# Gated loop attention with a SoLU feed-forward: float64 weights converted in 7 wide pieces instead of 14, with a new written order

## The chip, the cores and the metric

The kernel runs on one core of a Trainium2 chip. The metric is device time in microseconds, the median of several executions. A profile covers one execution; its span runs from the first to the last instruction.

## The reference, cut to what matters

Two blocks, one behind the other. The first is a recurrence over 768 steps for 4 batches and 8 heads of size 48, with a complex decay; its output, (4, 768, 384) after the heads are put side by side, is the input x (3072 rows of 384) of the second. The inputs of the second block, w_in, w_out and g_ln, arrive as float64.

```python
a_re_n, a_im_n = (a_re * scale, a_im * scale)      # magnitude held to 0.999
for t in range(S):
    new_re = ar * S_re - ai * S_im
    new_im = ar * S_im + ai * S_re
    S_re, S_im = (new_re + kv, new_im)             # kv: outer product of k and v at t
    y[:, :, t] = np.einsum('bhd,bhde->bhe', q[:, :, t], S_re)
...
h = x @ w_in                                       # (3072, 384) @ (384, 1024)
e = np.exp(h - h_max)
solu = h * (e / (np.sum(e, axis=-1, keepdims=True) + 1e-09))
ln = (solu - mu) / np.sqrt(var + 1e-06) * g_ln
return (ln @ w_out).astype(np.float32)             # (3072, 1024) @ (1024, 384)
```

## The kernel before

The work is cut into 24 chunks of 128 rows (6 stretches of time by 4 batches), taken in 12 groups of two. A fast path (`whole`, line 614) computes everything and a set of conditions; a flag of one number is read at the end (line 1289), and only if it is set a slower general program (`general`, line 57) runs as well. In the profile it does not run.

Each piece of work is a named step, and the text ORDER (line 515) lists all steps, name and number, in the order in which they are written into the program. Since every engine takes its instructions in the order written, ORDER fixes each engine's queue: a step that waits holds up all that is written behind it on its engine. Most steps give work to one engine:

- SP, the DMA queue: `load_ar`, `load_ai`, `load_q`, `load_k`, `load_v`, `load_vr` (inputs of a group), `fetch` (a piece of raw weights), `gain` (g_ln), `last` and `onward` (small rows carried on, lines 866 and 921), `kqt0` (line 972, four DMAs that finish the transpose of a chunk's k and q), `away` (line 1128, the same for the feed-forward's activations), `store`, and `again` (a second fetch of a piece).
- VectorE (DVE): `ratio`, `tangent`, `size`, `lnm`, `ks`, `qs`, `on`, the first half of `part`, `k2`, `q2`, `kqb` (block transpose), `mask0`, `add`, `solu0`, `blocks`, `convert`, `centre`, `inspect`, and `judge`, `judgew`, `judges`, `flag`.
- ScalarE (ACT): `inverse`, `sure`, `square`, `secant`, `fourth`, `eps`, `grow`, `decay`, `angle`, `nearest`, `sin`, `cos`, the table loads `trig` and `exp`, `turned_x`, `exp0`, `spread`, `scale`, `tot`, `raised`, the copies `kT`, `qT`, `zT` and the copy in `meansum`.
- TensorE (PE): `total` (f_L) and `phase`, both at line 852; `score`, `values` (f_y), `carry` (f_d), `up` (f_h, with w_in), `down` (f_o, with w_out), `mean` and `meansum`, the transposes `qt`, `kt`, `zt`, and `turn_ends` and `count`.
- GpSimd (POOL): `centred` and `norm`.

A group's chain is: load, inverse ... lnm, total, grow and decay, a table load, angle, phase, nearest, part, sin and cos, then for each of its chunks k2, q2, kqb, kqt0, score, mask0, values, turned_x, up, exp0, solu0, blocks, away, down, scale, store. Chunks 0, 1, 2 and 23 use TensorE transposes in place of some of the DMAs.

The weights: `weight_steps` (line 724) cuts w_in (128 partitions, 3 blocks of 1024 columns) and w_out (8 blocks of 384) into 14 pieces, 0 to 5 of 512 columns of w_in (0, 1, 2 the first halves) and 6 to 13 the blocks of w_out. `fetch` brings the 64-bit words into a ring of 6 raw tiles. `raised` (ScalarE, line 750) takes the low words into a tile `bits`, of which there are two; `convert` (VectorE, lines 756 to 760) makes float32 from the high words and `bits` with three instructions. `mean` needs every converted block of w_out, `centre` (line 784) rewrites w_out with g_ln and that mean, and `down` needs the centred blocks. Near the end `again` fetches every piece a second time into the same ring and `inspect` (line 763) takes the least magnitude of each, a column of `least`; `judgew` counts them. `judge` takes one tile of the ring as scratch.

## Time and profile before

| | us |
|---|---|
| median of 3 runs | 434.31 |
| lowest and highest run | 432.13, 434.33 |
| the profiled execution | 434.73 |
| its span | 432.9 |
| TensorE busy in the span | 385.3 (89%) |
| VectorE busy | 334.9 (77%) |
| ScalarE busy | 289.0 (67%) |
| GpSimd busy | 54.1 (12%) |

TensorE's busy time counts its matmuls, which are pipelined, with modelled ends, so a busy TensorE need not be at its peak. A row of a timeline gives start, length, engine, line, operation, output <- inputs and shapes, and in brackets the idle time of the engine before it with what ended it. In a row of waits the figures are the total, the number of times and the longest. "PE f_o L1166 x8" in the chain of waits stands for eight instructions of that line which the chain passes through.

### The profile page before, as it was taken

What the parts mean: (1) busy time and instruction counts of PE and PEld (TensorE: products, weight loads), DVE (VectorE), ACT (ScalarE), POOL (GpSimd) and SP (SyncE); (2) the same over time, 40 slices, a digit from 0 to 9 for tenths busy, and PEclk for the clock granted to TensorE, in tenths of its full rate; (3) what the DMA queues carried; (4) which work ended last, traced back from release to release, by engine and by line L of the source; (5) the groups of instructions that cost most, each with busy time, mean ns of one, the idle gap of its engine ahead of it and who ended that gap; (6) DMA issues with size and microseconds to landing.
All of it is one profiled execution on the core that took longest, in us unless ns stands there. A gap on an engine that the chain in (4) does not pass through costs nothing.

```text
span 432.9 us, 15841 instructions
## 1 busy us (share of the span) xinstructions
PE 385.3 (89%) x6928; PEld 216.6 (50%) x6928; DVE 334.9 (77%) x457; ACT 289.0 (67%) x475; POOL 54.1 (12%) x139
## 2 busy tenths in 40 slices
PE   0257697899999999999998999999999999999991
PEld 0024163555644554554644745545555777667550
DVE  3898979798697799698887697979787897971381
ACT  4998965897579578667676487865874866522340
POOL 3000100103003021011021021031022030120210
PEclk9999889999999999999999999999999999999996
DMA  9999476686776767947877689968868869689761
GB/s 210 277 243 198 116 104 143 141 138 150 179 136 144 172 144 175 191 89 153 174 143 154 169 166 210 179 135 194 161 135 190 163 144 198 140 212 283 218 202 34
DMA packets 168126, 72.59 MB, mean 168 GB/s; under 512 B 142576, under 2 KB 155888, under 8 KB 168048
## 3 DMA queue, kind: packets, MB, share of 16 engines
q1 hardware_dynamic: 167904, 71.17, 75.2%
q8 instruction: 56, 0.92, 0.9%
q10 hardware_dynamic: 144, 0.33, 0.3%
q14 instruction: 22, 0.18, 0.1%
HBM read 38.87 MB, written 4.72 MB: 101 GB/s over the span
## 4 chain that ended last, share of the span: by engine, by line
PE 58%; DVE 13%; DMA 12%; SPq 7%; ACT 5%; issue 3%; DVEq 0%; ACTq 0%
PE f_h L1089 19%; PE f_o L1166 19%; PE f_y L1048 7%; PE f_score L1015 5%; DMA f_raw<-in_moe_w_in_dram 4%; DVE f_kb L970 3%; PE f_phase L852 3%; SPq L1131 3%; PE f_d L1056 2%; DMA f_kqT<-f_kb 2%; SPq L975 2%; PE f_L L852 2%; DMA f_v<-in_v_dram 2%; DMA f_zT<-f_zb 2%; DVE f_kq L961 2%
## 5 line engine op out<-in xcount | busy, mean ns | idle before, releaser
L1166 PE MATMUL f_o<-f_w_out,f_zT 128*32 128x384 f32 (+1 forms) x1344 | 130.2, 486 | 2.7 <-DVE f_w_out L784 2.5
L1089 PE MATMUL f_h<-f_w_in,f_xT 128*32 128x512 f32 x1152 | 131.5, 593 | 1.2 <-ACT f_xT L1082 1.2
L1166 PEld LDWEIGHTS f_o<-f_w_out,f_zT 128*32 128x32 f32 (+1 forms) x1344 | 60.9, 114 | 62.1 <-issue 41.9
L1089 PEld LDWEIGHTS f_h<-f_w_in,f_xT 128*32 128x32 f32 x1152 | 47.3, 110 | 59.5 <-issue 53.2
L970 DVE STREAM_TRANSPOSE f_kb<-f_kq 128x1536 f32<-128x1536 f32 x22 | 55.4, 2518 | 2.4 <-DMA f_kqT<-f_kb 2.1
L1048 PE MATMUL f_y<-f_att,f_v 128*32 128x128 f32 (+1 forms) x384 | 37.9, 273 | 3.2 <-DMA f_v<-in_v_dram 1.8
L1082 ACT COPY f_xT<-f_y 128x384 f32<-128x384 f32 x24 | 11.4, 477 | 41.8 <-PE f_y L1048 41.8
L1015 PEld LDWEIGHTS f_score<-f_kqT 96*32 96x32 f32 x1536 | 33.5, 111 | 10.7 <-issue 9.3
L1108 DVE SCALAR_TENSOR_TENSOR f_z<-f_h,f_z 128x1024 f32<-128x1024 f32 (+1 forms) x36 | 33.7, 971 | 5.4 <-ACT f_z L1099 5.4
L1099 ACT ACTIVATE f_z<-f_h 128x1024 f32<-128x1024 f32 x24 | 29.3, 1219 | 11.5 <-PE f_h L1089 11.5
L1048 PE MATMUL f_y<-f_att,f_vr 128*32 128x128 f32 x384 | 36.8, 273 | 0.0
L1015 PE MATMUL f_score<-f_kqT 96*32 96x96 f32 (+3 forms) x1536 | 35.0, 236 | 0.7 <-ACT f_kqT L988 0.6
L1048 PE MATMUL f_y<-f_kqT,f_state 96*32 96x128 f32 (+1 forms) x640 | 34.3, 272 | 0.0
L852 PE MATMUL f_L<-f_lr,f_mats 128*32 128x384 f32 x192 | 20.0, 518 | 15.7 <-DMA f_vr<-in_v_dram 13.8
L1144 POOL TENSOR_SCALAR f_less<-f_sum 128x1 f32<-128x1 f32 x24 | 11.7, 489 | 174.1 <-DVE f_z L1108 173.8
L1020 DVE TENSOR_TENSOR f_att<-f_score,f_mats 128x1024 f32<-128x1024 f32 x24 | 29.2, 1216 | 5.1 <-PE f_score L1015 5.0
L1048 PEld LDWEIGHTS f_y<-f_att,f_v 128*32 128x32 f32 (+1 forms) x384 | 23.4, 103 | 12.8 <-issue 6.9
L1147 ACT ACTIVATE f_z<-f_z,f_less 128x1024 f32<-128x1024 f32 x24 | 27.4, 1143 | 1.7 <-POOL f_less L1144 1.6
L907 DVE SCALAR_TENSOR_TENSOR f_f<-f_f,f_phase 128x384 f32<-128x384 f32 x24 | 12.6, 552 | 18.9 <-ACT f_f L903 18.7
L852 PE MATMUL f_phase<-f_x,f_mats 128*32 128x384 f32 x192 | 21.0, 546 | 5.3 <-ACT f_x L890 5.3
L961 DVE TENSOR_TENSOR f_kq<-f_cs,f_k 128x768 f32<-128x768 f32 x24 | 22.8, 950 | 3.0 <-ACT f_cs L919 2.0
L1126 DVE STREAM_TRANSPOSE f_zb<-f_z 128x1024 f32<-128x1024 f32 x20 | 24.7, 1235 | 0.1
(101 smaller groups left out, 592.4 us busy)
## 6 DMA issues: line engine op xcount, KB each, us to landing
f_kqT<-f_kb SPq DMA_DIRECT2D x88, 192.0 KB, 3.6
f_zT<-f_zb SPq DMA_DIRECT2D x80, 128.0 KB, 3.2
f_raw<-in_moe_w_in_dram SPq DMA_DIRECT2D x12, 512.0 KB, 6.0
f_raw<-in_moe_w_out_dram SPq DMA_DIRECT2D x16, 384.0 KB, 5.3
f_q<-in_q_dram SPq DMA_DIRECT2D x12, 384.0 KB, 6.6
f_k<-in_k_dram SPq DMA_DIRECT2D x12, 384.0 KB, 4.9
f_v<-in_v_dram SPq DMA_DIRECT2D x12, 384.0 KB, 5.9
out_dram<-f_ot SPq DMA_DIRECT2D x24, 192.0 KB, 3.9
```

The costliest lines, as they stand in the source:

```text
L852: nc.tensor.matmul(out=ps[r:r + 32], lhsT=weights[:, r:r + 32], rhs=st[nm][:, i * DM:(i + 1) * DM], start=True, stop=True)
L961: nc.vector.tensor_tensor(out=t, in0=T["cs", g][:, i * H:(i + 1) * H], in1=heads(T[nm, g][:, i]).unsqueeze(2).to_broadcast([P, H, 2, D]), ...
L970: nc.vector.transpose(out=t, in_=T["kq", c].rearrange("p n h (f j) -> p j (n h) f", j=3))
L1015: nc.tensor.matmul(out=scores[r0:r0 + 32, x, r:], lhsT=QK[:, r // 32, x], rhs=QK[:, r // 32:, H + x], start=True, stop=True)
L1020: nc.vector.tensor_tensor(out=st["att"].rearrange("p (i u) t -> p i u t", u=2), in0=scores.rearrange("p (i u) t -> p i u t", u=2), in1=mat ...
L1048: nc.tensor.matmul(**product)
L1089: nc.tensor.matmul(out=st["h"][r:r + 32, half * 512:(half + 1) * 512], lhsT=st["xT"][:, c * P + r:c * P + r + 32], rhs=w_in[:, c, half * 5 ...
L1099: nc.scalar.activation(out=z, in_=h, func=AF.Exp, accum_out=sums[:, n:n + 1])
L1108: nc.vector.scalar_tensor_tensor(out=z, in0=h, scalar=1.0, in1=z, op0=OP.mult, op1=OP.mult, accum_out=st["sum"][:, 2 + i:3 + i])
L1126: nc.vector.transpose(out=st["zb"], in_=st["z"].rearrange("p (c s f) -> p s c f", s=4, f=32))
L1147: nc.scalar.activation(out=st["z"], in_=st["z"], func=AF.Square, bias=st["less"], accum_out=st["sum"][:, 1:2])
L1166: nc.tensor.matmul(out=st["o"][rows], lhsT=zT, rhs=w_out[:, c], start=(c == 0), stop=(c == KF - 1))
```

## The change

The 14 pieces become 7: pieces 0 to 2 are the whole blocks of w_in (1024 columns), 3 to 6 are pairs of blocks of w_out (768 columns, fetched by two DMAs into the two halves of one tile). The ring has 3 tiles of twice the size, and there is one `bits` tile of twice the size, so the memory is the same. `least` has 7 columns and `inspect` runs 7 times. ORDER is another text: not only the places of `fetch`, `raised`, `convert`, `again` and `inspect` are new, but also those of many other steps through the whole program.

```diff
-    rawp, bits = pool("f_raw", 6), pool("f_bits", 2)
+    rawp, bits = pool("f_raw", 3), pool("f_bits", 1)
...
-        NW = 512
+        NW = 1024
         pieces = []
-        for w, src, nk in ((w_in, moe_w_in, KD), (w_out, moe_w_out, KF)):
+        for w, src, nk, per in ((w_in, moe_w_in, KD, 1), (w_out, moe_w_out, KF, 2)):
             wide = src.bitcast(I32).rearrange("(c p) w -> p c w", p=P)
-            nf = w.shape[2]
-            for f0 in range(0, nf, NW):
-                for c in range(nk):
-                    pieces.append((w, wide, c, f0, min(NW, nf - f0)))
+            for c in range(0, nk, per):
+                pieces.append((w, wide, c, per, per * w.shape[2]))
 
         def fetch(i):
-            w, wide, c, f0, n = pieces[i % len(pieces)]
-            raw = rawp.tile([P, NW, 2], I32, tag="raw", name="f_raw")[:, 0:n]
-            rows = wide[:, c, 2 * f0:2 * (f0 + n)]
-            if w is w_out:
-
-                rows = rows.rearrange("(s f) x -> f s x", s=4)
-            nc.sync.dma_start(out=raw.rearrange("p n u -> p (n u)"), in_=rows)
-            T["raw", i] = raw
+            w, wide, c, per, n = pieces[i % len(pieces)]
+            raw = T["raw", i] = rawp.tile([P, NW, 2], I32, tag="raw", name="f_raw")[:, 0:n]
+            for k in range(per):
+                rows = wide[:, c + k]
+                if w is w_out:
+
+                    rows = rows.rearrange("(s f) x -> f s x", s=4)
+                m = n // per
+                nc.sync.dma_start(out=raw[:, k * m:(k + 1) * m].rearrange("p n u -> p (n u)"), in_=rows)
...
-            hi, x = T["raw", i][:, :, 1], w[:, c, f0:f0 + n].bitcast(I32)
+            hi, x = T["raw", i][:, :, 1], w[:, c:c + per].rearrange("p c w -> p (c w)").bitcast(I32)
```

The order, engine by engine, where the prediction speaks of it (steps of other names left out):

```diff
 SP, first 45 us
-fetch:0 fetch:10 fetch:1 fetch:4 load_vr:0 fetch:3 load_q:0 load_k:0 fetch:2 load_ar:1 load_ai:1 fetch:5 fetch:11 fetch:9 fetch:7 gain:0 load_v:0 fetch:13 fetch:12 last:0 load_k:1 load_q:1 load_v:1 fetch:6 fetch:8 onward:0
+fetch:5 fetch:1 load_k:0 fetch:0 load_q:0 fetch:2 load_vr:0 load_ar:1 load_ai:1 fetch:6 last:0 load_v:0 fetch:3 fetch:4 gain:0 onward:0 load_k:1 load_q:1 load_ar:2
 SP, groups 6 to 8
-kqt0:12 away:10 load_vr:6 load_k:7 load_v:6 kqt0:13 last:7 store:8 store:9 onward:6 away:11 ... kqt0:14 load_vr:7 away:12 onward:7 load_k:8 load_v:7 kqt0:15 ... kqt0:16 onward:8 away:14 load_vr:8 load_k:9 load_v:8 kqt0:17
+kqt0:12 store:6 load_vr:6 away:10 load_v:6 load_k:7 store:8 kqt0:13 last:7 onward:6 away:11 ... kqt0:14 onward:7 store:10 away:12 load_vr:7 load_v:7 load_k:8 load_ar:9 kqt0:15 ... kqt0:16 load_vr:8 away:14 load_v:8 load_k:9 kqt0:17 onward:8
 DVE, up to mask0:1
-sizea:0 convert:10 lnma:0 convert:1 convert:0 qs1:0 convert:3 ks1:0 part0:0 ks0:0 qs0:0 part1:0 convert:4 k2:0 q2:0 k2:1 q2:1 ratio:1 convert:11 tangent:1 mask0:0 convert:2 size:1 convert:5 convert:13 convert:12 lnm:1 convert:9 convert:7 ks1:1 qs0:1 ks0:1 qs1:1 solu0:0 convert:6 part1:1 part0:1 convert:8 mask0:1
+sizeb:0 convert:5 lnmb:0 convert:1 ks1:0 convert:0 part0:0 qs0:0 qs1:0 part1:0 ks0:0 q2:0 k2:0 q2:1 convert:2 k2:1 ratio:1 mask0:0 tangent:1 convert:6 size:1 convert:3 lnm:1 convert:4 ks1:1 ks0:1 qs0:1 solu0:0 part0:1 part1:1 mask0:1
 ACT, from exp:1 to the copy of the mean
-exp:1 meansum:0 inverse:2 zT1:0 turned_x:1
+exp:1 zT1:0 inverse:2 turned_x:1 meansum:0
 PE, from carry:1 to phase:2
-carry:1 score1:1 zt1:0 mean:0 mean:3 score0:1 mean:4 mean:2 ... mean:5 meansum:0 values:1 zt0:0 turn_ends:1 carry:0 up1:1 up0:1 down0:0 score1:2 score0:2 total1:2 down1:0 total0:2 values:2 zt1:1 zt0:1 carry:2 phase1:2
+carry:1 phase0:1 phase1:1 score1:1 score0:1 zt1:0 mean:0 mean:1 mean:3 values:1 mean:7 ... mean:6 turn_ends:1 meansum:0 carry:0 up0:1 zt0:0 up1:1 score0:2 score1:2 down0:0 total1:2 total0:2 down1:0 values:2 zt0:1 carry:2 phase1:2
 DVE, the end
-solu0:23 inspect:10 inspect:7 inspect:6 inspect:12 judges:0 inspect:9 inspect:5 judge:0 inspect:4 inspect:1 judgew:0 flag:0
+solu0:23 inspect:1 inspect:3 inspect:0 judgew:0 flag:0
```

181 lines of the change are left out of this document (89 added, 92 removed).

## The prediction

> **What bounds the kernel now.** I read first the busy time by stage, then the chain of waits, then the timeline around the weight conversion and at the end. The stages, with columns PE, PEld, DVE, ACT, POOL busy, granted clock, DMA share and GB/s:
>
> ```profile
> 0.00:13.70 13.70, 0.00 (x0) 0.00 (x0) 5.63 (x18) 7.87 (x16) 3.48 (x11) 1.00 0.96 240
> 13.70:70.00 56.30, 38.67 (x518) 18.62 (x518) 50.56 (x89) 46.07 (x81) 1.54 (x4) 0.94 0.84 176
> 70.00:85.00 15.00, 11.52 (x192) 7.17 (x196) 13.21 (x22) 12.05 (x20) 1.90 (x6) 1.00 0.65 132
> 85.00:235.00 150.00, 149.84 (x2819) 78.77 (x2814) 124.71 (x149) 109.68 (x180) 20.73 (x52) 1.00 0.74 154
> 235.00:335.00 100.00, 97.49 (x1938) 53.82 (x1934) 80.77 (x95) 68.81 (x111) 14.51 (x31) 1.00 0.80 170
> 411.00:432.90 21.90, 11.74 (x90) 6.70 (x82) 10.24 (x31) 5.92 (x8) 1.80 (x7) 0.83 0.38 120
> ```
>
> From 85 us on TensorE is the bound: 0.16 us idle in 150. What a reordering can win lies where TensorE idles: 13.7 us before its first matmul, 17.6 us in the stage that holds the conversions (56.30 less 38.67), 3.5 us from 70 to 85 (15.00 less 11.52), 2.5 us from 235 to 335, and the end. Between 13.7 and 70 VectorE is the fullest engine (50.56 of 56.30), so conversion instructions there are near the path.
>
> The stage from 235 to 335 costs more than its idle time says, as the chain shows (start, length, what):
>
> ```profile
> 87.05 5.20 PE f_h L1089 x48
> ...
> 209.62 2.56 PE f_h L1089 x21
> ...
> 324.76 7.39 DMA f_v<-in_v_dram
> ...
> 336.98 2.63 PE f_h L1089 x22
> ```
>
> These are the first matmuls with w_in of chunks 2, 10 and 18: eight chunks took 122.6 us, the next eight 127.4. 4.8 us more for the same matmuls, and the chain names a load of v just ahead of the end of it.
>
> **The change part by part.**
>
> Conversion and inspection, per instruction:
>
> ```profile
> L750 ACT ACTIVATE f_bits<-f_raw x14: 539/601/712, 14.3 to 52.2; 128x384 int32<-128x384 uint32 x8, 128x512 int32<-128x512 uint32 x6
> L763 DVE TENSOR_REDUCE f_least<-f_raw x14: 541/606/760, 384.8 to 422.4; 128x1 f32<-128x384 f32 x8, 128x1 f32<-128x512 f32 x6
> ...
> L756 DVE TENSOR_SCALAR f_w_out<-f_raw x8: 352/352/358, 15.0 to 55.9; 128x384 int32<-128x384 int32 x8
> L758 DVE SCALAR_TENSOR_TENSOR f_w_out<-f_raw,f_w_out x8: 557/560/566, 15.3 to 56.3; 128x384 int32<-128x384 int32 x8
> L756 DVE TENSOR_SCALAR f_w_in<-f_raw x6: 417/420/425, 17.0 to 39.5; 128x512 int32<-128x512 int32 x6
> L758 DVE SCALAR_TENSOR_TENSOR f_w_in<-f_raw,f_w_in x6: 691/693/720, 17.4 to 39.9; 128x512 int32<-128x512 int32 x6
> ```
>
> From 384 to 512 columns L756 grows by 68 ns, 0.53 ns a column, with 0.15 us fixed; L758 by 133 ns, 1.04 ns a column, with 0.16 us fixed. The third instruction (L760) I take like L758. So a piece of 512 costs 0.42+0.69+0.69 = 1.81 us, one of 384 1.47, and by the same slopes (estimates, the sizes are not in this trace) 768 costs 0.56+0.96+0.96 = 2.48 and 1024 costs 0.69+1.22+1.22 = 3.14. All conversions: 6 x 1.81 + 8 x 1.47 = 22.6 before, 3 x 3.14 + 4 x 2.48 = 19.3 after, 3.3 us less on VectorE. If the larger forms have no fixed part to save it is 0. On ScalarE, 14 instructions between 0.54 and 0.71 become 7 that I estimate at 0.85 and 1.05: about 1.9 us less. Of the 14 inspections (0.54 to 0.76), near the end, 7 are left, each twice as wide: about 1.2 us less.
>
> DMAs: a w_in piece is now one transfer of twice the size, a w_out piece two transfers as before, so both rounds together issue 22 instead of 28. It moves the same bytes. In the first 13.7 us the DMA engines are 0.96 busy at 240 GB/s with the small pieces, so I put the bandwidth gain at 0. The Trainium skill (DMA: Bandwidth & Descriptors, Rules for kernel authors) asks for at least 1 MiB a transfer, and puts about 2.0 us of fixed time on each (Anatomy of one DMA); were that paid in series, the three w_in transfers that go would be worth 6 us and the sum would be lower by that. By the 0.96 row that time is already overlapped, so the sum holds nothing of it.
>
> *Up to the first w_in matmul: 0.* Before, what stands on VectorE ahead of what feeds up:0 is conversions 10, 1, 0, 3, 4, 11, 2: two of 384 and five of 512, 11.99 us. After, it is 5, 1, 0, 2: 2.48 + 3 x 3.14 = 11.90. The chain of group 0 beside them (total, grow, phase, k2, q2, scores, mask) has the same steps. So the start of up stays:
>
> ```profile
> 39.28 1.07 PE L1089 MATMUL f_h<-f_w_in,f_xT 128*32 128x512 f32 x8 [1.16 <-ACT f_xT L1082]
> ```
>
> The unknowns are the new waits. The ring is three tiles, so fetch:2, 6, 3 and 4 wait for conversions 5, 1, 0 and 2. SP is in order: behind fetch:2 stand load_vr:0, load_ar:1, load_ai:1; behind fetch:6 last:0 and load_v:0; behind fetch:4 gain, onward:0, load_k:1, load_q:1 and load_ar:2. And there is one bits tile, so each raised on ScalarE waits for the convert before it; behind raised:1 stand grow, decay, trig and angle of group 0. The tightest is raised:1. In the old run the second half of group 0 gets its size and its eps here:
>
> ```profile
> 14.48 0.56 DVE L840 SCALAR_TENSOR_TENSOR f_lr<-f_u,f_lr 128x384 f32<-128x384 f32 x1 [0.77 <-ACT f_u L833]
> 15.72 0.61 ACT L844 ACTIVATE f_u<-f_u,f_bias 128x384 f32<-128x384 f32 x1
> ```
>
> In the new order convert:5 follows that size: 15.04 + 2.48 = 17.5. On ScalarE raised:5 (0.85) is put ahead of eps, and fourthb comes behind it before raised:1: 16.33 + 0.85 and a little = 17.2 to 17.9. So raised:1 asks for the tile about when it comes free; for the later ones the same walk finds VectorE up to 1.8 us early. I take 0; the bounds are -2 (half of the 3.3 us saved there and some of the fetch issues) and +5 (two waits of a whole conversion of 2.5).
>
> *From there to 70 us: 0.* Left to convert after up:0's inputs are 1.81 + 6 x 1.47 = 10.6 before and 3 x 2.48 = 7.4 after. Before, the last one ends among the phase steps of group 1, and mask0:1 waits for score0:1, which in PE's order stands behind matmuls of the mean, and these wait for it:
>
> ```profile
> 56.88 0.56 DVE L760 CUSTOM_DVE_ANT_0 f_w_out<-f_w_out,f_bits 128x768 uint16<-128x768 uint16 x1
> 59.03 1.22 DVE L1020 TENSOR_TENSOR f_att<-f_score,f_mats 128x1024 f32<-128x1024 f32 x1 [1.59 <-PE f_score L1015]
> ```
>
> After, all conversions stand ahead of part0:1, and score0:1 ahead of every mean; mask0:1 can start near 56.2, 2.8 us earlier. But the next w_in matmuls do not follow it, for ScalarE loads its table for exp:1 (first row; the second is that matmul):
>
> ```profile
> 58.20 1.28 ACT L950 ACT_TABLE_LOAD   x1
> ```
>
> ```profile
> 64.05 0.62 PE L1089 MATMUL f_h<-f_w_in,f_xT 128*32 128x512 f32 x1
> ```
>
> That load is not moved, and the new order puts zT1:0, inverse:2 and turned_x:1 ahead of the copy of the mean, so I find up0:1 near 64 again. The lead is lost here.
>
> *70 to 85 us: -2.4.* The old chain:
>
> ```profile
> 75.97 0.73 PE f_L L852 x8
> 76.69 2.78 PE f_o L1166 x8
> 79.47 0.83 PE f_L L852 x8
> 81.21 1.28 ACT L947
> 82.60 0.66 issue
> 83.77 0.88 PE f_d L1056 x48
> 84.65 1.32 PE f_phase L852 x16
> ```
>
> Half of the running sums of group 2 (f_L) stood behind down1:0 (2.78 us), and both halves go before the table load, the angle and the phase matmuls. The new order has total1:2 and total0:2 together ahead of down1:0, so the phase comes up to 2.8 us earlier while down1:0 fills TensorE. I take off 0.4 for a wait that opens before zt0:1. Bounds 0 and -3.5, the stage's whole idle time.
>
> *85 to 335 us: -1.5.* Waits of TensorE for others in this stretch, and ScalarE's at its worst place:
>
> ```profile
> PE f_y L1048 <- DMA f_v<-in_v_dram: 1.8, 2, 1.2
> ```
>
> ```profile
> 244.14 1.05 ACT L903 ACTIVATE f_f<-f_phase,f_bias 128x384 f32<-128x384 f32 x2 [3.74 <-DMA f_on<-f_f]
> ```
>
> In the old SP order load_v stood behind load_k of the next group (groups 6 to 9), which nobody needs so soon; in the new one load_v goes ahead, so v lands one transfer sooner. And onward:6, for whose transfer ScalarE waited 3.74 us, no longer stands behind store:9, and store:8 has gone ahead of kqt0:13. I take 1.5 of the 4.8 us, most of the named 1.8. The rest of the order is new as well and no row prices it: bounds -4.8 (all gone) and +4.8 (as much again).
>
> *The end: -0.2.*
>
> ```profile
> 423.87 0.34 SPq L1175 DMA_DIRECT2D out_dram<-f_ot  x1
> 424.01 0.14 DVE L1223 TENSOR_SCALAR flag<-f_total 1x1 int32<-1x1 f32 x1
> ```
>
> Before, the last inspection waits for its fetch, and the flag is ready at 424.15, next to the last store, which is issued at 423.87 after matmuls that the change leaves alone. After, only inspections 1, 3 and 0 (about 3.3 us) stand behind solu0:23 on VectorE, so the flag comes with or before the store. The store hides what more is saved.
>
> Sum: 434.73 (the profiled execution; span 432.9 and 1.83 around it) - 2.4 - 1.5 - 0.2 = 430.63. That execution is 0.42 above the median of the runs, 434.31, so I predict **430.2 us**.
>
> **The rivals.** *The lead is used up* (no change). The slow stage may be set by VectorE, SP and transfers that take their time in turn and not by TensorE; then its excess grows from 4.8 by the 2.4 won before: 434.31 - 0.2 = 434.1. For it: VectorE is 81 of 100 us busy there, and the chain passes through transfers. Against: TensorE is still 97.5 of 100.
>
> *Single buffering bites* (slower). If VectorE runs more than about 2 us behind my walk, ScalarE stops at raised, SP at fetch, and what stands behind them goes late. Two such stops of a whole conversion (2.5 to 3.1 us) are 5.4: 434.3 - 2.6 + 5.4 = 437.1. It decides where those margins, 0 to 1.8 us, are used up. For it: VectorE is 50.56 of 56.30 busy. Against: conversions are 3.3 us shorter. The Trainium skill (Trainium Kernel Development and Optimization, Best Practices) asks to double-buffer so that DMA and compute overlap, and the change goes from six and two tiles to three and one; by that rule this rival is the outcome.
>
> *Onward comes late* (slower). In the new SP order onward:1, 4, 5, 6, 8 and 9 stand behind the second kqt0 of their own pair of chunks, where before only onward:6 did. The one 3.74 us wait stood at the head of the 4.8 us excess. If two more such waits come, 434.3 - 2.6 + 9.6 = 441.3. It decides when the transfer lands after the next group's phase matmuls. Against: those matmuls stand behind a whole down and values, so I find the transfer about level with them.
>
> **How the numbers follow.** About 0.5% (2.2 us) is what a measurement of this kernel can tell from no change: faster is below 432.1, slower above 436.5. Forecast, with its own range of 427 to 432.1: 0.53. Lead used up: 0.22. Single buffering: 0.13. Onward late: 0.12. The first alone is faster and the last two are slower: 0.53, 0.22, 0.25. The lower end is 426.5: the forecast with the bounds -3.5 and most of -4.8. The upper end takes in the lead used up and single buffering, 437.5; the late onward and a little below the range are left out.
>
> **What would show it.** Right: 7 groups of conversions near 2.5 and 3.1 us; first w_in matmul at 39 to 40; chunk 1's between 63 and 65; phase of group 2 near 82; first w_in matmuls of chunk 2 near 84.5 instead of 87.05; chunks 10 to 18 in about 126; flag before the last store. Wrong: waits of f_bits for L760 above 1 us, SP idle at L743 in the first 45 us, the first w_in matmul later than 41, waits of L903 for f_on at more than one place, or TensorE idle over 3 us between 85 and 411.

## The result and the profile after

| | before | after |
|---|---|---|
| median of 6 runs, us | 434.05 | 423.58 |
| lowest and highest run | 432.13, 434.60 | 421.44, 424.28 |
| the profiled execution | 434.73 | 421.44 |
| its span | 432.9 | 419.1 |

The ratio is 0.9757 (95% interval 0.9724 to 0.9789): 10.5 us faster, where 4.1 were predicted. The time lies under the lower end of the range, 426.5. The two profiled executions are 13.3 us apart, since that of after is 2.1 us under its median; the last experiment looks at what goes with that.

The same stages of the changed kernel, with the columns PE, PEld, DVE, ACT, POOL, granted clock, DMA share, GB/s; the last row is again the last 21.9 us:

```profile
0.00:13.70 13.70, 1.05 (x8) 0.20 (x8) 6.24 (x20) 8.89 (x18) 3.48 (x11) 1.00 0.93 248
13.70:70.00 56.30, 39.20 (x584) 20.31 (x581) 52.99 (x74) 49.33 (x80) 0.61 (x3) 0.94 0.78 185
70.00:85.00 15.00, 14.99 (x239) 7.28 (x242) 12.46 (x21) 11.70 (x19) 3.54 (x7) 1.00 0.68 145
85.00:235.00 150.00, 149.81 (x2822) 79.83 (x2817) 124.98 (x149) 109.73 (x181) 23.85 (x53) 1.00 0.71 159
235.00:335.00 100.00, 100.00 (x2066) 54.19 (x2063) 84.52 (x97) 72.35 (x116) 15.59 (x33) 1.00 0.78 171
397.20:419.10 21.90, 14.62 (x118) 6.90 (x110) 6.60 (x18) 5.40 (x8) 2.56 (x9) 0.94 0.43 153
```

TensorE no longer idles from 70 to 85 (14.99 of 15, before 11.52) nor from 235 to 335 (100.00, before 97.49). From 13.7 to 70 it is hardly busier, 39.20 against 38.67, yet it does 584 matmul records instead of 518 in that time.

Four rows of its timeline answer to those of before: the first w_in matmuls of chunk 0, the phase of group 1, ScalarE's table load for exp:1, and the first w_in matmul of chunk 1.

```profile
38.86 5.36 PE L1085 MATMUL f_h<-f_w_in,f_xT 128*32 128x512 f32 x48 [0.35 <-ACT f_xT L1078]
...
50.16 1.50 PE L848 MATMUL f_phase<-f_x,f_mats 128*32 128x384 f32 x16 [1.08 <-ACT f_x L886]
...
55.03 1.28 ACT L946 ACT_TABLE_LOAD   x1
...
60.80 0.62 PE L1085 MATMUL f_h<-f_w_in,f_xT 128*32 128x512 f32 x1
```

The first stands where it stood (39.28 before); the table load has gone from 58.20 to 55.03 and the last row from 64.05 to 60.80. In the chain of waits chunks 2 and 18 begin w_in here:

```profile
80.04 5.15 PE f_h L1085 x48
...
324.96 2.57 PE f_h L1085 x22
```

Before it was 87.05 and 336.98. With "up n" for the first w_in matmul of chunk n, read from each trace, the stretches are:

| stretch | before | after | change | predicted |
|---|---|---|---|---|
| start to up 0 | 39.3 | 38.9 | -0.4 | 0 |
| up 0 to up 1 | 24.8 | 21.9 | -2.8 | 0 |
| up 1 to up 2 | 22.8 | 19.1 | -3.8 | -2.4 |
| up 2 to up 18 | 249.9 | 244.9 | -5.0 | -1.5 |
| up 18 to the last scale | 86.5 | 87.2 | +0.7 | 0 |
| last scale to the end of the span | 9.7 | 7.1 | -2.5 | -0.2 |

Two of these changes depend on which executions are compared. With the same instructions on the way, up 0 to up 1 took 24.0 to 24.8 us in the four traces with 14 pieces and the old start, and 21.9 to 23.1 in the five with seven pieces and the new one; up 2 to up 18 took 247.3 to 249.9 in five traces with the old order there and 244.8 to 248.1 in eight with the new. So the two gains lie anywhere from 0.9 to 2.9 us and from nothing to 5. Up 1 to up 2 is steady in the new order, 18.9 to 19.1 us wherever the edit does not touch it.

The conversions themselves came out as estimated. By instruction (min/median/max in ns):

```profile
L746 ACT ACTIVATE f_bits<-f_raw x7: 892/949/1160, 13.0 to 43.5; 128x768 int32<-128x768 uint32 x4, 128x1024 int32<-128x1024 uint32 x3
L752 DVE TENSOR_SCALAR f_w_out<-f_raw x4: 550/554/556, 13.6 to 44.3; 128x768 int32<-128x768 int32 x4
L754 DVE SCALAR_TENSOR_TENSOR f_w_out<-f_raw,f_w_out x4: 957/959/982, 14.2 to 44.9; 128x768 int32<-128x768 int32 x4
L754 DVE SCALAR_TENSOR_TENSOR f_w_in<-f_raw,f_w_in x3: 1224/1225/1226, 17.3 to 29.4; 128x1024 int32<-128x1024 int32 x3
```

0.55 and 0.96 us for 768 columns (estimated 0.56 and 0.96), 1.225 for 1024 (estimated 1.22). ScalarE's `raised` is up to 0.1 longer than estimated (0.85 and 1.05), so it saves 1.1 us in all and not 1.9.

### The profile page after: what moved, and what is told of

It is laid out like the page before. It is cut to its first block, busy times and chain, and to the rows that moved or that the text cites. A ratio compares the mean times of both kernels' runs of the same rounds, so it can differ in the third digit from the quotient of the medians.

```text
span 419.1 us, 15795 instructions
## 1 busy us (share of the span) xinstructions
PE 381.9 (91%) x6928; PEld 200.4 (48%) x6928; DVE 331.8 (79%) x429; ACT 287.5 (69%) x468; POOL 57.0 (14%) x139
## 4 chain that ended last, share of the span: by engine, by line
PE 79%; ACT 9%; DMA 4%; DVE 3%; issue 2%; SPq 0%; POOL 0%; DVEq 0%; ACTq 0%; POOLq 0%
PE f_o L1162 28%; PE f_h L1085 26%; PE f_y L1044 9%; PE f_score L1011 5%; PE f_phase L848 4%; PE f_L L848 4%; PE f_d L1052 3%; DMA f_ar<-in_a_re_dram 2%; DMA f_raw<-in_moe_w_out_dram 1%; DMA f_kqT<-f_kb 1%; PE f_zt L1112 1%; ACT f_cs L912 1%; ACT L946 1%; DVE f_kb L966 1%; ACT f_cs L907 1%
## 5 line engine op out<-in xcount | busy, mean ns | idle before, releaser
L1162 PEld LDWEIGHTS f_o<-f_w_out,f_zT 128*32 128x32 f32 (+1 forms) x1344 | 55.0, 114 | 64.9 <-issue 55.0
L1085 PEld LDWEIGHTS f_h<-f_w_in,f_xT 128*32 128x32 f32 x1152 | 39.7, 110 | 64.8 <-issue 64.0
L1044 PE MATMUL f_y<-f_att,f_v 128*32 128x128 f32 (+1 forms) x384 | 36.1, 273 | 1.2 <-DVE f_att L1016 1.2
L1140 POOL TENSOR_SCALAR f_less<-f_sum 128x1 f32<-128x1 f32 x24 | 13.1, 546 | 163.4 <-DVE f_z L1104 152.7
L1011 PE MATMUL f_score<-f_kqT 96*32 96x32 f32 (+3 forms) x1536 | 32.8, 236 | 0.0
L1044 PE MATMUL f_y<-f_kqT,f_state 96*32 96x128 f32 (+1 forms) x640 | 32.7, 272 | 0.0
L1166 ACT ACTIVATE f_ot<-f_o,f_rs 128x384 f32<-128x384 f32 x24 | 13.7, 573 | 16.5 <-POOL f_rs L1151 6.0
L1044 PEld LDWEIGHTS f_y<-f_att,f_v 128*32 128x32 f32 (+1 forms) x384 | 21.8, 103 | 6.2 <-issue 3.8
L1122 DVE STREAM_TRANSPOSE f_zb<-f_z 128x1024 f32<-128x1024 f32 x20 | 24.8, 1238 | 0.1
L957 DVE TENSOR_TENSOR f_kq<-f_cs,f_q 128x768 f32<-128x768 f32 x24 | 22.9, 952 | 2.2 <-ACT f_cs L912 1.1
```

The lines of the kernel that those rows point to most:

```text
L957: nc.vector.tensor_tensor(out=t, in0=T["cs", g][:, i * H:(i + 1) * H], in1=heads(T[nm, g][:, i]).unsqueeze(2).to_broadcast([P, H, 2, D]), ...
L1011: nc.tensor.matmul(out=scores[r0:r0 + 32, x, r:], lhsT=QK[:, r // 32, x], rhs=QK[:, r // 32:, H + x], start=True, stop=True)
L1044: nc.tensor.matmul(**product)
L1085: nc.tensor.matmul(out=st["h"][r:r + 32, half * 512:(half + 1) * 512], lhsT=st["xT"][:, c * P + r:c * P + r + 32], rhs=w_in[:, c, half * 5 ...
L1122: nc.vector.transpose(out=st["zb"], in_=st["z"].rearrange("p (c s f) -> p s c f", s=4, f=32))
L1162: nc.tensor.matmul(out=st["o"][rows], lhsT=zT, rhs=w_out[:, c], start=(c == 0), stop=(c == KF - 1))
```

## The experiments

The median of the kernel before, taken again beside each set of runs, was 432.5 to 433.2.

### Pieces and order apart

Four kernels take one part of the change each, first the pieces or the order, then the start or the rest of the order. The first has the old 14 pieces with the new order, each step of a wide piece written as the steps of its two old pieces:

```diff
 # kernel before, new_order_14
-ORDER = (old text)
+ORDER = (new text, fetch:0 as fetch:0 fetch:3, convert:3 as convert:6 convert:7, ...)
```

> The new written order with the old 14 narrow pieces: each wide step of the new order stands as its two halves one behind the other, ring of 6, two bits tiles. If the order makes the gain and the widths hardly matter (theory), it comes within 2 us of the changed kernel, 422 to 426 us, with chunk 2's first w_in matmul at 80 to 82. If the widths make the start (rival: 3.3 us less conversion work on VectorE, one by one on the path), the first 85 us lose 3 us or more and the time is 427 or above.

```diff
 # kernel after, old_order_7
-ORDER = (new text)
+ORDER = (old text, one step of each wide piece where the old ones stood)
```

> The old order with the 7 wide pieces, ring of 3 and one bits tile; each wide step stands where the first of its halves stood, a few moved back so that the ring and the bits tile are free. If the order makes the gain, 432 to 436 us, or slower where the old places don't suit wide pieces. If the widths make it, 427 or below.

```diff
 # kernel after, start_new_rest_old
+ORDER = (new text through values:3, then what is left in the order of the old text)
```

> Wide pieces; the new order up to values of chunk 3, everything left in the old order. If the start and the middle gain each for itself (theory), the start's 7 us are kept, chunk 2's first w_in matmul is at 80 to 81, chunks 10 to 18 take about 127 again, and the time is 427 to 429. If the middle's gain only follows from the early start (rival), chunks 10 to 18 take about 123 and the time is 423 to 425. If the old middle eats the lead, 432 or more.

```diff
 # kernel before, start_old_rest_new
+ORDER = (old text through values:3, then what is left in the order of the new text; 14 pieces)
```

> 14 pieces; the old order up to values of chunk 3, everything left in the new order. If start and middle gain each for itself, chunk 2's first w_in matmul stays near 87, chunks 10 to 18 take 122 to 124 and the time is 428 to 430. If the middle's gain only follows from the early start, chunks 10 to 18 take 127 and the time is 433 to 435.

| kernel | median | ratio to before, 95% | up 0 | up 1 | up 2 |
|---|---|---|---|---|---|
| new order, 14 pieces | 429.80 | 0.9927 (0.9889 to 0.9966) | 41.2 | 64.6 | 83.5 |
| old order, 7 pieces | 440.49 | 1.0157 (1.0125 to 1.0188) | 44.6 | 72.8 | 97.3 |
| new start, old rest, 7 pieces | 427.03 | 0.9832 (0.9779 to 0.9885) | 39.1 | 61.9 | 80.9 |
| old start, new rest, 14 pieces | 432.86 | 0.9984 (0.9958 to 1.0010) | 39.1 | 63.1 | 85.9 |

The two halves do not add. The wide pieces cost 7 us in the old order and bring 6 in the new one (429.80 to 423.58); the new order alone brings 3.4. Most of it is decided in the first 85 us: the new start with the old rest has 6.1 of the 10.5. The order alone thus missed its forecast of 422 to 426. The rest of the new order took 0.3 us off behind the old start (433.17, the median of before beside these four, to 432.86) and 3.4 behind the new one (427.03 to 423.58).

In the old order with seven pieces the trace shows the stops of the rival "single buffering bites". ScalarE's timeline:

```profile
17.44 1.16 ACT L746 ACTIVATE f_bits<-f_raw 128x1024 int32<-128x1024 uint32 x1 [1.22 <-DVE f_w_out L756]
21.14 1.16 ACT L746 ACTIVATE f_bits<-f_raw 128x1024 int32<-128x1024 uint32 x1 [2.53 <-DVE f_w_in L756]
...
27.78 0.58 ACT L899 ACTIVATE f_f<-f_phase,f_bias 128x384 f32<-128x384 f32 x1 [1.21 <-PE f_phase L848]
```

Two stops at the one `bits` tile, 3.75 us, ahead of the angle of group 0; `nearest0:0` comes at 27.8. In the changed kernel it comes at 22.7, and all its stops for that tile before 70 us are one row of the waits:

```profile
ACT f_bits L746 <- DVE f_w_out L756: 0.7, 1, 0.7
```

The Trainium skill (Trainium Kernel Development and Optimization, Best Practices) asks for double buffers; in these two traces the single one makes ScalarE wait 3.75 us ahead of that angle where the order leaves no slack at it, and 0.7 us where the order was written for it.

A fifth kernel took the two stops out of the old order:

```diff
 # old order with 7 pieces: four steps moved behind the chain of group 0
-... raised:5 sizea:0 convert:5 epsa:0 raised:1 lnma:0 convert:1 total1:0 load_vr:0 raised:0 ... load_q:0 convert:0 ... trig:0 anglea:0 ... angleb:0 phase0:0 nearest0:0
+... raised:5 sizea:0 convert:5 epsa:0 lnma:0 total1:0 load_vr:0 ... trig:0 raised:1 convert:1 anglea:0 ... angleb:0 raised:0 phase0:0 convert:0 nearest0:0
```

> The old order with the seven wide pieces (440.5 us), with raised:1, convert:1, raised:0 and convert:0 moved behind ScalarE's trig and angle steps of group 0, about where the new order has them. Theory (single buffering costs through its stops): ScalarE stood 1.22 and 2.53 us at raised for the one bits tile, ahead of the angle of group 0, and without these two stops the phase of group 0 comes 3 to 4 us earlier, first w_in matmul at 41 to 41.7 instead of 44.6, time 436.5 to 437.5. Rival: the loss of the old order comes from the ring of three raw tiles and from wide conversions ahead of later steps; then the first w_in matmul stays within 0.8 of 44.6 and the time at 440.

440.08 us, ratio 1.0141 (1.0069 to 1.0214): no gain that can be told from nothing. The phase of group 0 came 2.9 us earlier (23.3 for 26.2) and up 0 1.7 earlier (42.9), but up 1 stayed at 72.6. So these two stops are not the price of the old order. Its trace has more of the same kind behind them. SP waits for a conversion before it may fetch into the ring of three, VectorE then waits for that fetch, and ScalarE waits again for the one `bits` tile:

```profile
SPq L740 <- DVE f_w_in L754: 10.2, 2, 9.4
...
48.08 0.56 DVE L752 TENSOR_SCALAR f_w_out<-f_raw 128x768 int32<-128x768 int32 x1 [3.03 <-DMA f_raw<-in_moe_w_out_dram]
...
50.77 0.90 ACT L746 ACTIVATE f_bits<-f_raw 128x768 int32<-128x768 uint32 x1 [2.19 <-DVE f_w_out L756]
```

The conversion at 48.08 stands ahead of what feeds the running sums of group 1, which begin at 51.8 there and at 44.5 in the changed kernel. That these waits are the rest of the price was not tried by a run.

### The prediction's terms alone

```diff
 # kernel after, total0_behind_down
-total1:2 exp0:1 total0:2 kqb:3 decay0:2 grow1:2 load_k:3 grow0:2 mask0:2 add:0 decay1:2 trig:2 down1:0 load_k:2 solu0:1
+total1:2 exp0:1 kqb:3 grow1:2 load_k:3 mask0:2 add:0 down1:0 decay1:2 total0:2 load_k:2 solu0:1 grow0:2 decay0:2 trig:2
```

> The changed kernel with the second half of group 2's running sums (total0:2) and its grow and decay behind down1:0 again, as the old order had them. My prediction's term for the stretch from 70 to 85 us, alone: phase of group 2 from 77.6 to 80 to 80.5, first w_in matmuls of chunk 2 from 79.9 to 82.3 to 82.7, time up by 2.4 to 2.8, to about 426.2. Rival: the stage is filled by other matmuls that TensorE takes first, so the term is worth under 0.8 and the time stays within 423.4 to 424.4.

425.27 us, ratio 0.9789 (0.9715 to 0.9862), 1.7 above the changed kernel. Up 1 to up 2 took 21.1 us instead of 19.1. (Up 0 to up 1 is later in this trace too, which the edit does not touch; see the last experiment.) Its chain shows the step as it was before:

```profile
73.85 0.78 PE f_L L848 x8
74.63 2.78 PE f_o L1162 x8
77.41 0.83 PE f_L L848 x8
...
79.15 1.28 ACT L943
```

So this term is right by the traces: 2.0 us, predicted 2.4. The median alone would not show it; the interval, 0.9715 to 0.9862, holds the changed kernel's 0.9757.

```diff
 # kernel before, onward_and_v
+onward:6 ahead of load_vr:6; load_v:g ahead of load_k:g+1 for g = 6, 7, 8, 9
```

> The kernel before with only five moves on SP: onward:6 ahead of load_vr:6, and load_v ahead of load_k for groups 6 to 9. My prediction's term for the stretch from 85 to 335 us: chunks 10 to 18 in 123 to 126 us instead of 127.4, time 1.5 us down, to about 431.7 (433.2 is the median of the kernel before). Rival: the 127.4 belonged to one execution and not to the order (four other kernels, one of them with the old order from there on, had 122.6 to 124.6); then chunks 10 to 18 take 123 to 124.5 in this one too, but the time stays at 433.2 within 0.7.

The prediction's move of store:8 is not among these five. 432.62 us against 432.54, ratio 0.9985 (0.9948 to 1.0022). Chunks 10 to 18 in the trace of before, and in this one:

```profile
209.40:336.80 127.40, 124.89 (x2505) 68.11 (x2495) 102.56 (x120) 88.44 (x145) 18.58 (x40) 1.00 0.80 167
```

```profile
208.80:332.80 124.00, 123.78 (x2506) 64.40 (x2498) 102.52 (x120) 89.10 (x145) 18.01 (x40) 1.00 0.82 169
```

TensorE's idle time there falls from 2.51 to 0.22 us, which is what the step said. But the time of ten runs does not show it.

The kernel before was then profiled once more, unchanged:

> The kernel before once more, unchanged, for a second profile. Theory (the 127.4 us of chunks 10 to 18 belonged to one execution): this one has 122.5 to 125 there, and a span near 429 to 430. Rival (it belongs to the old order): 126.5 to 128 again. The half clock of TensorE around the phase of group 1 (0.50 from 52 to 56 us) should be there again if it comes from the gap ahead of it, phase 2.0 to 2.8 us instead of 1.5.

435.44 us (one run), span 433.6; chunks 10 to 18 in 126.2 us with 1.8 idle. So the slow stretch is not that of one execution, against the theory. Yet three kernels with the old rest and seven pieces had 123.8 to 124.6. What the stretch is worth in the median stays open.

### What became of the lead from 39 to 61 us

The prediction had conversions 2.8 us earlier and then put the gain at nothing. First, one conversion of the changed kernel goes back among the phase steps of group 1:

```diff
 # kernel after, convert4_late
-exp0:0 convert:4 total1:1 ... phase1:1 nearest1:1 part0:1
+exp0:0 total1:1 ... phase1:1 nearest1:1 convert:4 part0:1
```

> The changed kernel with one conversion (convert:4, 2.48 us on VectorE) put back where the old order had its last two, among the phase steps of group 1 (just ahead of part0:1). Theory: the gain of the first 80 us came from conversions that no longer stand between the phase of group 1 and its last exp, so the table load of ScalarE (58.20 before, 55.03 after) moves back by most of 2.5 us, to 56.5 to 57.5; first w_in matmul of chunk 1 at 62 to 63.3 instead of 60.8, of chunk 2 at 81 to 82.5 instead of 79.9; time 425 to 426. Rival: the table load went earlier for the order of TensorE (scores ahead of the means) and of ScalarE alone; then nothing moves: load at 55.0, time 423.6.

423.50 us, ratio 0.9761 (0.9684 to 0.9838). In the trace the table load is 1.16 later (56.19), up 1 1.2 and up 2 1.1; the median cannot tell that from nothing. One third of the 3.2 us, then, by the trace.

More was in a column that the prediction had not read by the microsecond: the granted clock. Two windows before the phase of group 1 and two behind it, in the kernel before:

```profile
48.00:50.00 2.00, 0.64 (x4) 0.39 (x4) 2.00 (x5) 1.98 (x5) 0.00 (x0) 1.00 0.03 8
50.00:52.00 2.00, 0.11 (x4) 0.11 (x8) 2.00 (x8) 1.99 (x4) 0.00 (x0) 0.53 0.07 14
52.00:54.00 2.00, 2.00 (x16) 0.67 (x19) 1.83 (x7) 1.26 (x3) 1.19 (x3) 0.50 1.18 219
54.00:56.00 2.00, 2.00 (x67) 1.55 (x60) 1.28 (x5) 1.09 (x4) 0.36 (x2) 0.50 1.40 194
```

and in the changed kernel:

```profile
48.00:50.00 2.00, 1.07 (x51) 0.76 (x49) 2.00 (x7) 1.99 (x2) 0.00 (x0) 1.00 0.02 3
50.00:52.00 2.00, 1.84 (x47) 1.07 (x51) 1.12 (x5) 1.43 (x4) 0.61 (x3) 1.00 0.76 156
52.00:54.00 2.00, 1.37 (x50) 1.07 (x38) 1.91 (x3) 1.88 (x4) 0.00 (x0) 1.00 1.14 225
```

Before, TensorE has 0.75 us of work from 48 to 52, the clock falls to 0.50, and it stays there to 57: 16 phase matmuls take 2.79 us where the changed kernel needs 1.50.

```profile
51.89 2.79 PE L852 MATMUL f_phase<-f_x,f_mats 128*32 128x384 f32 x16 [2.38 <-ACT f_x L890]
```

How long it lasts differs. In before_again, with the same instructions, the fall is half as long:

```profile
50.00:52.00 2.00, 0.04 (x4) 0.04 (x6) 2.00 (x7) 1.99 (x4) 0.00 (x0) 0.96 0.06 11
52.00:54.00 2.00, 2.00 (x16) 0.67 (x19) 1.83 (x7) 1.28 (x3) 1.10 (x3) 0.50 1.23 223
54.00:56.00 2.00, 2.00 (x84) 1.55 (x79) 1.27 (x5) 1.11 (x3) 0.44 (x2) 0.69 1.41 189
```

The clock records of the traces give the stretches at 0.50 exactly: 50.1 to 57.0 us in before (6.83 us) and 51.8 to 55.2 in before_again (3.41). In all nineteen traces the clock changes only at points that lie a whole number of 3.41 us apart, and where these points fall differs from one execution to the next. All five traces with 14 pieces, the old start and no added matmuls have such a fall here, and up 1 at 63.1 to 64.1.

In the new order `carry:1` stands in the gap as well: between the sums and the phase (46.0 to 50.2) TensorE has about 1.5 us of work, and the clock is 1.00 through the phase. It is not safe for good: in the traces of split_again (an edit of the end, further below) and start_new_rest_old, with the same instructions up to there, it fell behind the phase (0.50 from 55.2 to 58.7 and from 55.4 to 58.8), and up 1 came at 61.9 instead of 60.8. The Trainium skill (TensorE: Matmul & The Clock Gate, What's actually happening) says that the clock goes to half after about 3.4 us of idleness and comes back after as long a busy stretch. Both agree, within such steps: the fall comes in a gap of 4.8 us (47.1 to 51.9) with 0.64 us of work in it, and the return after 5.1 us of matmuls in before and 3.3 in before_again.

Two causes are thus named for one stretch, and each was taken out of the kernel before alone, then both:

```diff
 # kernel before, warm_phase: matmuls that nobody reads, in front of phase1:1
+            if g == 1 and i == 1:
+                w = ps_t.tile([P, DM], FP, tag="t", padded_shape=[P, 512], name="f_warm")
+                for u in range(2):
+                    running(w, u, tri, "lr")
             ps = st["phase", i] = ps_t.tile(...)
```

> The kernel before with 16 matmuls added whose result nobody reads (group 1's running sums once more, 1.5 us), just ahead of the phase of group 1, in the gap in which TensorE had only 0.75 us of work from 48 to 52 us. Theory: the gap made the clock fall to 0.50, and that is one of two causes for the first w_in matmul of chunk 1 being 3.2 us later than in the changed kernel. With the filler the clock stays at 1.00 and the phase takes 1.5 us instead of 2.8; but the conversion in VectorE's line still ends at 54.1, so the table load comes only 0.5 to 0.9 earlier (57.3 to 57.7) and the time falls by 0.5 to 1. Rival: the filler is too short for the clock, nothing changes.

```diff
 # kernel before, short_6_8: in convert(i), behind the first instruction
+            if i in (6, 8):
+                return
```

> The kernel before with the second and third instruction of conversions 6 and 8 left out (2.2 us less on VectorE, among the phase steps of group 1; two of fourteen pieces of the weights are then not converted). Theory: the other cause is VectorE's conversions, but as long as the phase runs at half clock its first half ends near the same time, so this alone moves the table load by at most 0.6 and the time by 0 to 0.7. Rival (VectorE alone sets it): load at 56.5 to 57.0 instead of 58.2, first w_in matmul of chunk 1 at 62 to 62.6, time down by 1.2 to 1.8.

and both edits in one kernel, warm_and_short:

> Both of the two edits above in the kernel before (filler matmuls, and two conversions cut to their first instruction). Theory (two causes side by side, each hides the other): together they give more than the sum of the two, table load at 56.2 to 56.8 instead of 58.2, first w_in matmul of chunk 1 at 61.9 to 62.6, time 1.5 to 2.2 us under the kernel before. Rival: no more than the larger of the two alone.

| kernel | median | ratio, 95% | phase matmuls, us | table load at | up 1 | up 2 |
|---|---|---|---|---|---|---|
| before | 432.97 | | 2.79 | 58.20 | 64.0 | 86.9 |
| filler matmuls | 430.58 | 0.9937 (0.9891 to 0.9983) | 1.50 | 57.39 | 62.5 | 84.7 |
| two conversions cut | 432.81 | 1.0002 (0.9963 to 1.0041) | 2.79 | 58.22 | 64.1 | 86.9 |
| both | 430.05 | 0.9946 (0.9905 to 0.9987) | 1.50 | 56.90 | 62.0 | 84.4 |

With the fillers:

```profile
50.00:52.00 2.00, 1.05 (x16) 0.26 (x12) 2.00 (x8) 1.99 (x4) 0.00 (x0) 1.00 0.09 16
52.00:54.00 2.00, 2.00 (x75) 1.22 (x74) 1.83 (x7) 1.90 (x4) 1.12 (x3) 1.00 1.23 223
```

```profile
51.87 1.50 PE L852 MATMUL f_phase<-f_x,f_mats 128*32 128x384 f32 x16 [0.95 <-ACT f_x L890]
...
54.10 1.01 DVE L911 SCALAR_TENSOR_TENSOR f_f<-f_f,f_phase 128x384 f32<-128x384 f32 x2
```

1.5 us of matmuls that compute nothing make the old kernel 2.4 us faster, more than the 0.5 to 1 that was expected. (One of their ten executions took 2290 us; it counts in the median, not in the ratio, no trace of it was kept, and why is open. Without it the median is 430.40.) The table load moves by only 0.81 us, because VectorE reaches `part` at 54.10 as before (54.08), behind conversion 6; up 1 is then 1.5 and up 2 2.2 us earlier than in the trace of before. Against onward_and_v and start_old_rest_new, where the fall was the short one, it is 0.6 to 0.7 and 1.2 to 1.4 us. With the conversions cut alone nothing moves at all, since half the phase is ready no earlier than 54.1:

```profile
54.11 0.55 DVE L909 SCALAR_TENSOR_TENSOR f_f<-f_f,f_phase 128x384 f32<-128x384 f32 x1 [1.24 <-ACT f_f L905]
```

Only behind the fillers does the trace show another 0.5 us at the load, up 1 and (0.2) up 2; the medians, 430.58 and 430.05, cannot tell it. That is the picture of two waits side by side: as long as the clock falls, it hides the conversions.

The other way round, VectorE was made slower in the changed kernel:

```diff
 # kernel after, convert_twice: first two instructions of convert
+            for _ in range(2 if i in (3, 4) else 1):
```

> The changed kernel with the first two instructions of conversions 3 and 4 done twice (3.04 us more on VectorE between 40 and 47 us, the same result). Theory: between the first w_in matmul and group 1's phase VectorE's conversions are on the path, so the 3.2 us that the wide pieces and the shorter remainder saved there are what brought the phase forward; then the phase of group 1 comes 2.5 to 3 us later (50.2 to 52.7 to 53.2), first w_in matmul of chunk 1 at 63.3 to 63.8 instead of 60.8, time 426 to 427. Rival: ScalarE (z, exps, table) or PE sets the phase there and VectorE has cover; then under 1 us and 423.6 to 424.4.

426.27 us, ratio 0.9816 (0.9747 to 0.9884), 2.7 above the changed kernel, as the theory has it. Its trace does not prove the theory, though: the profiled execution has up 0 at 40.4, ahead of the edit, and the same start of the running sums of group 1 (47.03) as the execution of total0_behind_down, in which no conversion was longer. The interval holds the changed kernel's 0.9757, too. So this run decides nothing; and the clock fell again ahead of the phase (0.71 and 0.50 from 52 to 56), up 1 at 66.0.

### The exit, and the size of the transfers

The exit is what follows the last scale: the last store, the flag, the branch on it, and some twenty instructions on SP that wait for the other engines and end the program. In the kernel before SP does nothing for 2.18 us in the middle of these, in the changed one for 0.06 at the same place. Its three DRAIN instructions show it, spread over 2.5 us in before and 0.4 in after:

```profile
L1318 SPq DRAIN  x3: 7/13/130, 429.9 to 432.4; - x3
```

```profile
L1314 SPq DRAIN  x3: 7/7/13, 418.3 to 418.7; - x3
```

In all eight traces with 14 pieces this stand is 1.6 to 2.7 us, always behind SP's 472nd instruction (counted in the records of the trace). SP has 476 to 482 instructions in them, and at most 469 in the changed kernel and its edits up to here.

```diff
 # kernel after, split_again: second round only, w_in pieces in four transfers
-                nc.sync.dma_start(out=raw[:, k * m:(k + 1) * m]..., in_=rows)
+                for h in range(4) if w is w_in and i >= len(pieces) else (None,):
+                    ...
```

> The changed kernel with each of the three w_in pieces of the second round (those that are only inspected, after 384 us) fetched in four transfers: 9 more instructions on SP, none on the way to anything but the inspections. Theory: in all six profiled kernels with fourteen pieces SP stands 1.6 to 2.7 us behind its 472nd instruction, at the very end, and in none of the kernels with seven pieces, whose SP has at most 469; with 478 the stand comes back, last scale to end 9 to 10 us instead of 7.1, time about 425.6 to 426. Rival: the stand belongs to something else in the fourteen pieces (inspections, waits for transfers); then last scale to end stays at 7.0 to 7.4 and the time at 423.6.

```diff
 # kernel after, split_first: first round only, w_in pieces in two transfers
+                for h in range(2) if w is w_in and i < len(pieces) else (None,):
+                    ...
```

> The changed kernel with each of the three w_in pieces of the first round fetched as two transfers of 512 KB instead of one of 1 MB; conversions unchanged. Theory (transfers overlap, their size is worth nothing): first w_in matmul at 38.9 within 0.5 and the time within 423 to 424.5, unless the 472nd instruction of SP now falls inside the kernel. Rival (the fixed time of a transfer counts): first w_in matmul 1 to 4 us later.

split_again: 425.36 us, ratio 0.9802 (0.9738 to 0.9865), 478 instructions on SP; behind the 472nd it stands 2.15 us, and last scale to end takes 9.3 us instead of 7.1. split_first: 422.18, ratio 0.9762 (0.9697 to 0.9828), 472 instructions, no stand, 7.0 us; up 0 at 38.5. The two medians do not settle it, for both intervals hold 0.9757; the traces do.

So the stand goes with the number of SP's instructions and not with the width of the pieces, the inspections or the flag. The packets of queue 14, of the kind "instruction", for before, after and split_again (packets, MB, share):

```profile
q14 instruction: 22, 0.18, 0.1%
```

```profile
q14 instruction: 21, 0.17, 0.1%
```

```profile
q14 instruction: 22, 0.18, 0.1%
```

One packet more where SP goes past that place (two of the nine traces with the stand have only 21; records can be missing). But in the trace of before that packet starts at 432.73 us, when the stand is over (429.89 to 432.07); the one ahead of it ends at 429.87, just as the stand begins. So it is not seen to be what SP waits for. That SP stands because its next instructions are missing is a guess that fits the count, and is not shown. The Trainium skill (Runtime: NRT & Kernel Launch, Instruction fetch mechanics) says that instructions come in blocks, mostly hidden, but that a taken branch breaks the prefetch; the stand comes 11 to 17 instructions behind the branch on the flag.

And the transfers: two of 512 KB in place of each of 1 MB cost nothing that shows, as the sum had it (up 0 at 38.5, against 38.9 with the large ones). The 2.0 us for each transfer that the prediction took from the Trainium skill (DMA: Bandwidth & Descriptors, Anatomy of one DMA) are stated there for DMAs issued from GpSimd; these are issued from SP, and no such time shows in the start.

### Why the runs of the changed kernel lie 3 us apart

```diff
 # kernel after, after_warm: 8 matmuls that nobody reads ahead of phase0:0, 16 behind phase1:0
+            if g == 0 and i == 0:
+                T["warm"] = ps_h.tile([P, FF], FP, tag="h", name="f_warm")
+                running(T["warm"][:, 0:DM], 0, tri, "lr")
 ...
+            if g == 0 and i == 1:
+                for u in range(2):
+                    running(T["warm"][:, 0:DM], u, tri, "lr")
```

> The changed kernel with 24 matmuls added whose result nobody reads (group 0's running sums), 8 ahead of the phase of group 0 and 16 behind it, in gaps of TensorE between 18 and 27 us. Theory: TensorE runs at half clock up to 34.5 us in one execution and to about 42 in another (32 score matmuls of 1.30 or 0.77 us, the first 48 w_in matmuls 6.67 or 5.36 us), and this is why the changed kernel's runs lie between 421.4 and 424.3; with the gaps filled the clock is full by 27, f_turned and scores at 27 to 35 take the shorter times, first w_in matmul at 37.8 to 38.7, the median at 421 to 422 and the spread smaller. Rival: DMA and ScalarE's order set these stretches, first w_in matmul within 0.3 of 38.9 and the median within 0.7 of 423.6.

and beside it the changed kernel unchanged, after_again:

> The changed kernel once more, unchanged, beside the one with fillers on the same chip. 423.6 median within 0.8, runs from 421 to 425; in its trace the first w_in matmul at 38.5 to 39.1 if the second score group takes 0.77 us, at 40.4 to 40.6 if it takes 1.30.

after_again: 423.05 us, ratio 0.9800 (0.9752 to 0.9847); its runs are 421.2, 421.7 and 421.8, and 424.3, 424.4 and 426.1. after_warm: 423.52, ratio 0.9791 (0.9738 to 0.9844), from 420.9 to 426.4: no gain. Of the twelve runs of the changed kernel five lie between 421.2 and 421.9, six between 424.0 and 426.1 and one, 423.1, between them. The traces show two kinds of start. Here the second group of scores and the first w_in matmuls, first in the trace of after (421.44 us), then in that of total0_behind_down (427.55), which has the same instructions up to there:

```profile
34.62 0.77 PE L1011 MATMUL f_score<-f_kqT 96*32 96x128 f32 x32
...
38.86 5.36 PE L1085 MATMUL f_h<-f_w_in,f_xT 128*32 128x512 f32 x48 [0.35 <-ACT f_xT L1078]
```

```profile
34.90 1.30 PE L1011 MATMUL f_score<-f_kqT 96*32 96x128 f32 x32
40.54 6.67 PE L1085 MATMUL f_h<-f_w_in,f_xT 128*32 128x512 f32 x48
```

In one TensorE is back at full speed at 34.2 us, in the other only after the first w_in matmuls have begun, and group 1's sums follow them 2.5 us later (44.49 and 47.03). The fillers, 4.2 us of matmuls between 18 and 26.4, did not help: in that trace the clock came to 1.00 at 26.1, fell to 0.50 again at 29.5 and came back only at 43.2, with up 0 at 40.7. (In after it was 1.00 from 24.0 to 27.4, 0.50 to 34.2, and 1.00 from there.)

Nine traces have this start with seven pieces. In six of them the clock is at 1.00 from 33.1 to 34.9 us on, in three (total0_behind_down, convert_twice, after_warm) only from 42.6 to 43.2 on. They sort by where the points fall at which the clock changes: modulo 3.41 us, at 1.6 to 2.3 in the three, and at 2.4 to 3.4 or under 0.8 in the six. So the place of these points, which no kernel here sets, may choose the kind; no run tries it. Nor is it shown that the slower runs of the changed kernel are the late kind, for both of its own traces (421.44 and 421.16) are of the early one, and split_again took 427.30 with an early start.

## Why the prediction was wrong, point by point

**Pieces and conversions.** Right, to 0.01 us an instruction on VectorE; `raised` saves 0.8 less than estimated.

**Up to the first w_in matmul: 0.** Right: -0.4. The walk along raised:1 found the tile about level; the wait is 0.7 us. Against 14 pieces in the same order up 0 is 2.3 us earlier: there 13.8 us of conversions stand ahead of it, 1.9 more (part of it may be the clock, since the second group of scores took 1.25 us in that trace and 0.77 in this).

**From there to 70 us: 0.** This is the step that failed. It carried 2.8 us of earlier conversions and gave them up with the sentence "That load is not moved". The load moved by 3.17 us between the two profiled executions, and up 1 with it by 3.25 (over all traces up 0 to up 1 gained 0.9 to 2.9). The mask itself ran at 52.88 instead of 59.03, 6.2 us earlier and not 2.8. The load is not an obstacle with a place of its own; it stands in ScalarE's queue behind sin, cos and phase of group 1, so the question was what sets the phase. The steps of the lead: group 1's sums 1.1 us earlier (44.49 for 45.62), the phase 1.7, the load 3.2. Between phase and load 1.4 us are gained, and for that two causes were shown in the old kernel, half clock and conversions 6 and 8: without both the two are 5.0 us apart, against 6.3 before and 4.9 after. What set the 1.7 us up to the phase stays open; the run meant for it, convert_twice, does not tell. Behind the load nothing more is gained (5.85 and 5.77 us to up 1).

**70 to 85 us: -2.4.** Right in the mechanism, 2.0 us when undone alone. The stretch gained 3.8; the other 1.8 were not taken apart.

**85 to 335 us: -1.5.** Right in the direction; 5.0 us between the two profiled executions, the wide end of what the traces give. The five moves on SP take TensorE's idle time away as foreseen and cannot be seen in the time.

**The end: -0.2.** Wrong: -2.5. The flag no longer mattered, as predicted, but the sum stopped at the flag and the last store, and over 8 us of exit lie behind them. There the change won 2 us because its fewer transfers leave SP 469 instructions instead of 476. The prediction counted these transfers, 22 for 28, and gave them no price. This is the second term that it put at nothing.

**The rivals.** "Lead used up" was wrong: the middle stage gave no lead back. "Single buffering bites" is seen in the waits of the wide pieces in the old order, which is 7 us slower, and not in the new. "Onward comes late" did not come: the same stage runs at 100.00 of 100.

**The median.** 434.73 - 13.3 is 421.4, an execution of the faster group of the changed kernel's runs; the median of all is 423.6. So of the 6.4 us by which the forecast fell short part is the lead (0.9 to 2.9), part the exit (2.3) and part the other 1.4 from up 1 to up 2; the rest is not taken apart.

## What to carry to other kernels

Before a gain is written off against a later step on another engine, follow that step's own queue back: if what stands ahead of it moves, it moves too. Read the granted clock by windows of 2 us wherever TensorE pauses for about 4 us; a gap costs its own length and then, here, 3.3 to 5.1 us of matmuls at half speed, and work put into the gap was worth more here than work taken away. Take more than one trace of the same kernel before a difference of 1 us in a stretch is explained. A written order and the number of its buffers are one choice: each of the two halves tried alone gave the wrong sign or a third of the effect.

## What the hardware showed that was not expected

- 1.5 us of added, useless matmuls made a kernel 2.4 us faster (0.9937, interval 0.9891 to 0.9983), and in its trace the clock stays at 1.00 where it had fallen to 0.50.
- The granted clock changes only at points a whole number of 3.41 us apart, which fall elsewhere in each execution. With the same instructions it comes back at about 34 us in some executions and at about 43 in others, and up 0 is then 1.7 us later (38.86 and 40.54). Fillers of 4.2 us did not choose the better kind.
- The clock column says 1.00 where the trace has no clock record. In total0_behind_down the first record begins at 43.2 us, and 32 score matmuls ahead of it take 1.30 us instead of 0.77; the durations are the surer sign there.
- SP stands 1.6 to 2.7 us behind its 472nd instruction, at the exit, in all nine traces of kernels that have more, and in none of the ten that have 472 or fewer.
